# The second layer's output product by seven products instead of eight, with its weight sums made in the kernel

## The chip, the cores and the metric

The kernel runs on one core of one Trainium2 chip. The metric is the device time of one execution in microseconds; the median of three runs is given. A profile of one execution comes with it.

## The reference

The input goes through an attention step, a gated layer and a second layer. The change touches the last product of the second layer only:

```python
def _moe2_ref(x, w_in, w_out, alpha) -> np.ndarray:
    h = x @ w_in
    g = np.maximum(h, 0.0) + alpha * np.minimum(h, 0.0)
    return (g @ w_out).astype(np.float32)
```

There are 2304 tokens (18 tiles of 128), 512 model columns and 2048 hidden columns. The product `g @ w_out` is 2304 x 2048 by 2048 x 512. Weights arrive as 64-bit floating-point numbers and are turned into 32-bit ones in the kernel.

## The kernel before, in words

**Precision.** Each operand is split into a high half in TensorE's fp32r type (a ScalarE copy) and a low half, value minus high half (a subtraction on GpSimd). Each product is three matmuls: high by high, high by low, low by high (`mm3`, L487 to L490).

**Layer 2's input product** already uses seven products in place of eight (Strassen's scheme, in Winograd's form). It runs in visits: each visit takes a block of 576 tokens and a run of weight pairs `q`, and there are 32 steps of one block and one pair. A step (`step`, `close`, `prod`) has seven products of six matmuls of 288 columns. Sums of products are formed by letting ScalarE copy a finished product from one PSUM bank into another, on which the next product accumulates. After it VectorE adds and applies the activation (`close`, `prelu`, L901, L902, L909), and SyncE stores the result in the DRAM buffer `hbuf`.

**Layer 2's output product** comes after the visits. `m2_out` takes groups: for the first eight token tiles one hidden row block of 128 after the other, then the next eight tiles, then the last two tiles with four row blocks at a time, 36 groups in all. `h_load` brings 512 KB of `hbuf` (L955), `h_split` makes high halves on ScalarE (L963) and low halves on GpSimd (L964). The eight PSUM banks hold one tile each. Every token tile takes 16 x 3 matmuls of 512 columns.

**The output weights** are converted by `conv_o(q)`, one pair of row blocks each: two loads (L104), two ScalarE passes that take the bits out (`bits` L662, `top` L666), one VectorE merge of both (L670), a high half on ScalarE (L745), a low half on GpSimd (L748). In the last visit a pair is issued after each step; the last one comes after the visits.

**The order.** From the last block of layer 1 on, every engine's order is written out by the kernel. A planner holds tasks (`bg`) with an engine, an estimated cost (`COST`), dependencies and a due time. After every few matmuls `tick` moves an estimated clock and `run_bg` emits the tasks that could start about then (`LA`, `LB`, `LBD` say how far ahead). `force` emits a task that a matmul needs now. `crit` books time for work on the path that the planner does not place. `A0` is the planned time of the first step. Each engine executes what it was given in that order, so an instruction that waits holds up those behind it.

Of the kernel before, what the change touches and what calls it, by code (L numbers as in the profile page):

```python
# [8 lines left out]
F32 = mybir.dt.float32  # L9
# [14 lines left out]
def attn_moe_moe2_kernel(  # L24
# [570 lines left out]
    COST = dict(A=lambda n: 0.2 + 0.00082 * n, D=lambda n: 0.16 + 0.0011 * n, P=lambda n: 0.05 + 0.0025 * n, S=lambda n: 8.0)  # L595

    def bg(eng, n, fn, *deps, at=0.0):
        t = dict(e=eng, d=COST[eng](n) * (1.25 if eng == "D" and due[0] < A0 + 20.0 else 1.0), fn=fn, deps=deps, at=at, end=None, due=due[0])
        tasks.append(t)
        tasks.sort(key=lambda x: x["due"])  # L600
        return t

    def run_bg(flush=False):
        now = clock[0]
        busy = set()
        for t in list(tasks):
            if not flush:
                if t["e"] in busy:
                    continue
                more = 0.8 if t["due"] < now + 6.0 else 0.0  # L610
                if t["at"] > now or any(d["end"] is None or d["end"] > now + LA + more for d in t["deps"]):
                    continue
                if t["e"] != "S" and free.get(t["e"], 0.0) > now + (LBD if t["e"] == "D" and now > A0 else LB) + more:
                    busy.add(t["e"])
                    continue
            start = max([now, 0.0 if t["e"] == "S" else free.get(t["e"], 0.0)] + [d["end"] for d in t["deps"]])
            t["end"] = start + t["d"] + 0.15
            if t["e"] != "S":
                free[t["e"]] = start + t["d"]
            tasks.remove(t)  # L620
            t["fn"]()

    def force(t):
        if t["end"] is None:
            for d in t["deps"]:
                force(d)
            start = max([clock[0], free.get(t["e"], 0.0)] + [d["end"] for d in t["deps"]])
            t["end"] = start + t["d"] + 0.15
            if t["e"] != "S":
                free[t["e"]] = start + t["d"]  # L630
            tasks.remove(t)
            t["fn"]()
# [15 lines left out]
    held = dict(st0=[], st2=[], st1=[], sk=[])  # L648
# [87 lines left out]
    def conv_o(q, at):  # L736
        due[0] = A0 + 179.2 + 11.0 * q
        s = PAIR[q]
        ops = []
        for e, home in ((0, s[2]), (1, s[3])):  # L740
            z, load, bits, top, merge = unpack("o2", 2 * q + e, s[3 + e], e)

            def hi(z=z, home=home):
                z["w"] = wp.tile([128, 2, 512], F32R, tag=home, name="w2")
                nc.scalar.copy(out=z["w"][:, 0], in_=z["st"])  # L745
# [5 lines left out]
            ops.append((load, bits, top, merge, hi, lo))  # L751
        ls = [bg("S", 0, o[0], at=at) for o in ops]
        for e, (_, bits, top, merge, hi, lo) in enumerate(ops):
            st = f"st{e}"
            b_ = bg("A", 512, bits, ls[e], *held[st])
            k_ = bg("A", 512, top, b_, *held["sk"])
            m_ = bg("D", 512, merge, b_, k_)
            h_ = bg("A", 512, hi, m_)
            o_ = bg("P", 512, lo, h_)
            held[st] = [h_, o_]  # L760
            held["sk"] = [m_]
            ot[2 * q + e] = o_
# [184 lines left out]
    GROUPS = [(0, 8, [j]) for j in range(F2)] + [(8, 8, [j]) for j in range(F2)] + [(16, 2, list(range(j, j + 4))) for j in range(0, F2, 4)]  # L947
    hraw = {}
    hspl = {}
    HR, HH, HL = [[f"y{m}" for m in YO[e:e + 2]] for e in (0, 2, 4)]  # L950
# [6 lines left out]
    def h_split(u, half):  # L957
        m0, nm, js = GROUPS[u]
        if half == 0:
            hspl[u] = [p2b.tile([128, len(js), nm * 128], F32R, tag=tags[u % 2], name="hs", bufs=1) for tags in (HH, HL)]  # L960
        h, l = [t.rearrange("p j t -> p (j t)")[:, 512 * half:512 * half + 512] for t in hspl[u]]
        r = hraw[u].rearrange("p j t -> p (j t)")[:, 512 * half:512 * half + 512]
        nc.scalar.copy(out=h, in_=r)  # L963
        nc.gpsimd.tensor_sub(l, r, f32(h))  # L964

    def m2_out(u, bank):
        m0, nm, js = GROUPS[u]
        gh, gl = hspl.pop(u)
        for m in range(nm):
            if u + 1 < len(GROUPS) and m in (0, nm // 2):  # L970
                h_split(u + 1, 0 if m == 0 else 1)
            if m == nm // 2 and u + 3 < len(GROUPS):
                h_load(u + 3)
# [5 lines left out]
            if js[-1] == F2 - 1:  # L979
                os_ = (side2.tile([128, 2, HB], F32, tag="t2", name="os2", bufs=3) if m < 3 or m > 5 else  # L980
                       side2.tile([128, 2, TB], F32, tag=("sy0", "sy1", "yP5")[m - 3], name="os2", bufs=1))
                os_ = os_.rearrange("p e c -> p (e c)")[:, 0:512]
                if m % 2:
                    nc.vector.tensor_copy(os_, bank[m])  # L984
                else:
                    nc.scalar.copy(out=os_, in_=bank[m])
                r0 = (m0 + m) * 128
                nc.sync.dma_start(out=out[r0:r0 + 128, :], in_=os_)

    if True:  # L990
# [258 lines left out]
```

## Time and profile before

| | us |
|---|---|
| runs: 991.93, 992.30, 994.86; median | 992.3 |
| the profiled execution | 992.76 |
| its span, first to last instruction | 991.0 |
| TensorE busy | 951.9 |
| VectorE, GpSimd, ScalarE busy | 493.1, 457.5, 382.2 |

The span is what the trace covers; the execution's own time is 1.76 us longer. A line number in the trace is a line of the kernel. Engines are PE (TensorE), PEld (its weight loads, which overlap), DVE (VectorE), ACT (ScalarE), POOL (GpSimd) and SP (SyncE). Matmuls are pipelined: the spacing of their starts, not their duration, is what one costs.

### The profile page before, as it was taken

What the parts mean: (1) busy time and instruction counts of PE and PEld (TensorE: products, weight loads), DVE (VectorE), ACT (ScalarE), POOL (GpSimd) and SP (SyncE); (2) the same over time, 40 slices, a digit from 0 to 9 for tenths busy, and PEclk for the clock granted to TensorE, in tenths of its full rate; (3) what the DMA queues carried; (4) which work ended last, traced back from release to release, by engine and by line L of the source; (5) the groups of instructions that cost most, each with busy time, mean ns of one, the idle gap of its engine ahead of it and who ended that gap; (6) DMA issues with size and microseconds to landing.
All of it is one profiled execution on the core that took longest, in us unless ns stands there. A gap on an engine that the chain in (4) does not pass through costs nothing. (4 is left out here: it accounts for less than half of the span.)

```text
span 991.0 us, 20390 instructions
## 1 busy us (share of the span) xinstructions
PE 951.9 (96%) x8144; PEld 881.6 (89%) x8144; DVE 493.1 (50%) x990; ACT 382.2 (39%) x876; POOL 457.5 (46%) x551
## 2 busy tenths in 40 slices
PE   5689989999999999999999999999999999999998
PEld 4578889999999999999999998999999877888886
DVE  5887875455444645354541465878677730010010
ACT  4698732222222222222221556544424663232231
POOL 6488862234322243322221398854510486454543
PEclk9989899999999999999999999999999999999999
DMA  7999731132110322111101634252426763353242
GB/s 191 273 332 339 175 92 27 36 80 56 37 48 17 65 62 47 39 22 23 40 17 43 200 109 157 108 181 103 161 97 235 254 215 107 103 173 105 87 130 104
DMA packets 151702, 116.22 MB, mean 117 GB/s; under 512 B 98873, under 2 KB 130617, under 8 KB 150841
## 3 DMA queue, kind: packets, MB, share of 16 engines
q1 hardware_dynamic: 151543, 114.92, 38.6%
q8 instruction: 63, 1.03, 0.4%
q14 instruction: 32, 0.26, 0.1%
q10 hardware_dynamic: 64, 0.01, 0.0%
HBM read 86.58 MB, written 34.60 MB: 122 GB/s over the span
## 5 line engine op out<-in xcount | busy, mean ns | idle before, releaser
L964 POOL TENSOR_TENSOR hs<-hr,hs 128x512 fp32r<-128x512 f32 x72 | 93.7, 1318 | 88.5 <-ACT hs L963 86.4
L488 PE MATMUL g<-xh,w 128*128 128x288 f32 x360 | 110.1, 306 | 7.8 <-DVE u L532 3.4
L532 DVE SCALAR_TENSOR_TENSOR u<-u,g 128x288 f32<-128x288 f32 x90 | 40.7, 453 | 148.2 <-ACT u L531 148.1
L488 PE MATMUL v<-xh,w 128*128 128x288 f32 x360 | 109.7, 305 | 0.0
L489 PE MATMUL v<-xl,w 128*128 128x288 f32 x360 | 109.5, 304 | 0.0
L490 PE MATMUL g<-xh,w 128*128 128x288 f32 x360 | 107.6, 299 | 1.2 <-POOL qT L294 1.2
L490 PE MATMUL v<-xh,w 128*128 128x288 f32 x360 | 107.8, 299 | 0.9 <-POOL w L143 0.9
L489 PE MATMUL g<-xl,w 128*128 128x288 f32 x360 | 107.7, 299 | 0.0
L489 PE MATMUL y<-pl,w 128*128 128x288 f32 x336 | 99.5, 298 | 0.4 <-POOL pl L547 0.4
L490 PE MATMUL y<-ph,w 128*128 128x288 f32 x336 | 98.9, 297 | 0.0
L547 POOL TENSOR_TENSOR pl<-u,ph 128x288 fp32r<-128x288 f32 x84 | 70.4, 838 | 59.0 <-ACT ph L546 58.6
L488 PE MATMUL y<-ph,w 128*128 128x288 f32 x336 | 97.5, 302 | 0.0
L963 ACT CAST hs<-hr 128x512 fp32r<-128x512 f32 x72 | 41.7, 617 | 111.0 <-PE y L489 99.3
L531 ACT ACTIVATE u<-g 128x288 f32<-128x288 f32 x90 | 36.9, 410 | 121.0 <-PE g L490 117.5
L984 DVE COPY os<-c 128x512 f32<-128x512 f32 x5 | 3.5, 692 | 154.6 <-PE c L490 154.6
L488 PEld LDWEIGHTS g<-xh,w 128*128 128x128 f32 x360 | 68.9, 191 | 10.0 <-DVE u L532 3.8
L546 ACT CAST ph<-u 128x288 fp32r<-128x288 f32 x84 | 36.3, 432 | 90.0 <-DVE u L539 90.0
L489 PEld LDWEIGHTS v<-xl,w 128*128 128x128 f32 x360 | 69.3, 193 | 1.7
L490 PEld LDWEIGHTS v<-xh,w 128*128 128x128 f32 x360 | 69.5, 193 | 1.2 <-POOL w L143 1.2
L490 PEld LDWEIGHTS g<-xh,w 128*128 128x128 f32 x360 | 69.1, 192 | 1.4 <-POOL qT L294 1.4
L488 PEld LDWEIGHTS v<-xh,w 128*128 128x128 f32 x360 | 69.3, 193 | 0.9 <-DVE u L539 0.3
L489 PEld LDWEIGHTS g<-xl,w 128*128 128x128 f32 x360 | 69.1, 192 | 0.0
(260 smaller groups left out, 2751.7 us busy)
## 6 DMA issues: line engine op xcount, KB each, us to landing
hbuf<-t SPq DMA_DIRECT2D x64, 288.0 KB
hr<-hbuf SPq DMA_DIRECT2D x36, 512.0 KB
raw<-in_moe_w_out_dram SPq DMA_DIRECT2D x28, 512.0 KB
raw<-in_moe_w_in_dram SPq DMA_DIRECT2D x16, 512.0 KB
raw<-in_moe_w_gate_dram SPq DMA_DIRECT2D x12, 512.0 KB
raw<-in_moe_w_val_dram SPq DMA_DIRECT2D x12, 512.0 KB
vw<-vwin SPq DMA_DIRECT2D x48, 96.0 KB
sy<-y SPq DMA_DIRECT2D x8, 576.0 KB
```

What stands on the lines that cost most here:

```text
L488: nc.tensor.matmul(o, lhi, rhi, start=first, stop=False)
L489: nc.tensor.matmul(o, lhi, rlo, start=False, stop=False)
L490: nc.tensor.matmul(o, llo, rhi, start=False, stop=last)
L531: nc.scalar.activation(out=u, in_=G[:, :HB], func=AF.Tanh, scale=0.5)
L532: nc.vector.scalar_tensor_tensor(out=u, in0=u, scalar=1.0, in1=G[:, :HB], op0=ALU.add, op1=ALU.mult)
L546: nc.scalar.copy(out=ph, in_=u)
L547: nc.gpsimd.tensor_sub(pl, u, f32(ph))
L963: nc.scalar.copy(out=h, in_=r)
L964: nc.gpsimd.tensor_sub(l, r, f32(h))
L984: nc.vector.tensor_copy(os_, bank[m])
```

## The change

The 18 token tiles are divided. Four tiles (0 to 3) keep the plain product, two row blocks at a time: `prep_h` and `plain`. The other 14 form seven groups of two tiles, 256 tokens each. A group's product is a two by two block product (token tile by token tile, even row block and odd row block of a pair, left and right 256 output columns) and is computed with seven products: `prep_g`, `gprod`, `group`, `gopen`, `gclose`. Each product runs over eight row pairs with three matmuls of 256 columns. Sums of products are seeded in PSUM by ScalarE copies, as in the visits; one VectorE addition remains for each group (`row2`).

The sums of weights are made from each converted pair (`sums`, `diffs`), and their halves too (`x1`, `x2`). The sums of h are made by VectorE in place in the loaded tile (`comb`: four on each half of the contraction, 128 x 512 each). High halves stay on ScalarE. A new task kind `"V"` goes to GpSimd up to one microsecond before `B0`, about the end of the visits, and to VectorE from then on; all low halves and sums of the output product are of this kind.

Memory comes from a list of free slots (`spare`, `take`), to which the last visit's steps hand over the slots of the weights that they have used up; at most eight raw loads and five split halves of groups are held at once (`CAP`). All eight weight pairs are given to the planner at the start of the last visit. The first plain unit is put before the last step's closing products, and group 0's first product before the last plain unit. In `run_bg` the look-ahead is zero from 4 us before `A0` to 3 us after it. `m2_out`, `h_load` and `h_split` go.

```diff
--- before.py
+++ after.py
...
+    B0 = A0 + 32 * 5.6 + 1.0
+    vec = [None]
+    spare = []
...
+    def engine(t):
+        e = t["e"]
+        if e == "V":
+            e = "P" if clock[0] < B0 - 1.0 else "D"
+        vec[0] = nc.gpsimd if e == "P" else nc.vector
+        return e, COST[e](t["n"]) * (1.25 if e == "D" and t["due"] < A0 + 20.0 else 1.0)
...
+    used = dict(raw=0, ring=0)
+    CAP = dict(raw=8, ring=5)
...
+    def run_bg():
         now = clock[0]
+        la, lb = (0.0, 0.0) if A0 - 4.0 < now < A0 + 3.0 else (LA, LB)
...
+            if t["at"] > now or t["need"] > room or any(d["end"] is None or d["end"] > now + la + more for d in t["deps"]):
...
+            if e != "S" and free.get(e, 0.0) > now + (LBD if e == "D" and A0 < now < B0 else lb) + more:
+                busy.add(e)
+                continue
...
-    def conv_o(q, at):
-        due[0] = A0 + 179.2 + 11.0 * q
-        s = PAIR[q]
...
-            def lo(z=z, j=2 * q + e):
-                nc.gpsimd.tensor_sub(z["w"][:, 1], z["st"], f32(z["w"][:, 0]))
-                WO[j] = z["w"]
...
-            h_ = bg("A", 512, hi, m_)
-            o_ = bg("P", 512, lo, h_)
...
+    NM = 4
+    NG = (NT // 128 - NM) // 2
+    TG = B0 + 11.0 * NM
...
+    def conv_o(q):
+        due[0] = B0 + 11.0 * NM * q / NQ - 4.0
+        z = {}
+        tag = ("sk", "st2")[q % 2]
...
+        def hi(k):
+            def go():
+                z["s" + k] = take([128, 2, 512], F32R, "w2")[0]
+                nc.scalar.copy(out=z["s" + k][:, 0], in_=z[k])
+            return go
+
+        def lo(k):
+            def go():
+                vec[0].tensor_sub(z["s" + k][:, 1], z[k], f32(z["s" + k][:, 0]))
+                if k[0] == "w":
+                    WO[2 * q + int(k[1])] = z["s" + k]
+                if k == "w1" and q % 2:
+                    spare.append(z["back"])
+                if k == "x2":
+                    spare.append(z["xback"])
+            return go
...
+        def sums():
+            x, z["xback"] = take([128, 2, 512], F32, "st")
+            z["x1"], z["x2"] = x[:, 0], x[:, 1]
+            (a, b), (c, d), (t1, t2) = pair("w0"), pair("w1"), pair("x1")
+            vec[0].tensor_sub(t1, b, a)
+            vec[0].tensor_sub(t2, d, t1)
+
+        def diffs():
+            (a, b), (c, d), (t1, t2), (t4, t3) = pair("w0"), pair("w1"), pair("x1"), pair("x2")
+            vec[0].tensor_sub(t3, d, b)
+            vec[0].tensor_sub(t4, c, t2)
...
+        l0 = bg("S", 5.5, load(0), *ld, at=B0 - 44.0, need=1)
+        l1 = bg("S", 5.5, load(1), *ld, at=B0 - 44.0, need=1)
+        b0 = bg("A", 512, bits(0), l0, *st[0], need=more)
+        k0 = bg("A", 512, top(0), b0, *held[tag])
+        m0 = bg("D", 512, merge(0), b0, k0)
+        b1 = bg("A", 512, bits(1), l1, b0, *st[1])
+        k1 = bg("A", 512, top(1), b1, m0)
+        m1 = bg("D", 512, merge(1), b1, k1)
...
+        h0 = bg("A", 512, hi("w0"), m0, need=1)
+        h1 = bg("A", 512, hi("w1"), m1, need=1)
+        o0 = bg("V", 512, lo("w0"), h0)
+        dA = bg("V", 600, sums, m0, m1, need=1)
+        dB = bg("V", 600, diffs, dA)
+        o1 = bg("V", 512, lo("w1"), h1, o0, dB)
...
+        due[0] = TG + 1.0 * q
+        hA = bg("A", 512, hi("x1"), dB, at=B0 - 3.0, need=1)
+        oA = bg("V", 512, lo("x1"), hA)
+        due[0] = TG + 8.0 + 1.0 * q
+        hB = bg("A", 512, hi("x2"), dB, at=B0 - 3.0, need=1)
+        oB = bg("V", 512, lo("x2"), hB, oA)
+        ot[2 * q], ot[2 * q + 1] = o0, o1
+        half = lambda k, h: lambda: (z["s" + k][:, 0, 256 * h:256 * h + 256], z["s" + k][:, 1, 256 * h:256 * h + 256])
+        OX[q] = dict(P1=half("w0", 0), P2=half("w1", 0), P3=half("w1", 1), P5=half("x1", 0), P6=half("x1", 1),
+                     P4=half("x2", 0), P7=half("x2", 1))
+        ox[q] = dict(P1=o0, P2=o1, P3=o1, P5=oA, P6=oA, P4=oB, P7=oB)
...
-    GROUPS = [(0, 8, [j]) for j in range(F2)] + [(8, 8, [j]) for j in range(F2)] + [(16, 2, list(range(j, j + 4))) for j in range(0, F2, 4)]
...
-    def h_load(u):
-        m0, nm, js = GROUPS[u]
-        t = hraw[u] = p2b.tile([128, len(js), nm * 128], F32, tag=HR[u % 2], name="hr", bufs=1)
-        nc.sync.dma_start(out=t, in_=hbuf[js[0] * 128:(js[-1] + 1) * 128, m0 * 128:(m0 + nm) * 128].rearrange("(j p) t -> p j t", p=128))
...
-        nc.scalar.copy(out=h, in_=r)
-        nc.gpsimd.tensor_sub(l, r, f32(h))
...
-    def m2_out(u, bank):
-        m0, nm, js = GROUPS[u]
...
-            for e, j in enumerate(js):
+    hs = {}
+    NJ = 8 // NM
+
+    def prep_h(u):
+        due[0] = B0 + 5.5 * u - 1.7
...
+        ld = bg("S", 5.5, load, at=due[0] - 16.0, need=1)
+        h0 = bg("A", 512, hi(0), ld, at=due[0] - 8.0, need=2)
+        h1 = bg("A", 512, hi(1), h0)
+        o0 = bg("V", 512, lo(0), h0)
+        o1 = bg("V", 512, lo(1), h1, o0)
...
+    def plain(u, bank):
+        z, done = hs[u]
+        force(done)
+        gh, gl = [t[0] for t in z["s"]]
...
-                nc.sync.dma_start(out=out[r0:r0 + 128, :], in_=os_)
+            if u == F2 // NJ - 1:
+                os_ = otile()
+                nc.scalar.copy(out=os_, in_=bank[m])
+                crit("A", 512)
+                nc.sync.dma_start(out=out[m * 128:(m + 1) * 128, :], in_=os_)
...
+    GT = 20.15
+    GO = ["P1", None, None, "P6", "P2", "P7", "P5", None, "P4", "P3"]
+    GL = ["P1", None, None, "P6", "P2", "P5", "P7", "P4", "P3"]
...
+    def prep_g(g):
+        tok = (NM + 2 * g) * 128
...
+                t, R[b][f"h{r}"] = take([128, 4, 256], F32, "hr")
+                nc.sync.dma_start(out=t, in_=hbuf.rearrange("(q r p) t -> r p q t", r=2, p=128)[r][:, 4 * b:4 * b + 4, tok:tok + 256])
+                R[b][f"1{r + 1}"] = t[:, :, 0:128]
+                R[b][f"2{r + 1}"] = t[:, :, 128:256]
+            return go
...
+                zs[m, b] = t, _ = take([128, 2, 4, 128], F32R, "hs")
+                nc.scalar.copy(out=t[:, 0], in_=R[b][SRC[m]])
...
+                vec[0].tensor_sub(t[:, 1], R[b][SRC[m]], f32(t[:, 0]))
...
+        def when(m, b):
+            return TG + GT * g + (GT / 7) * ((GO if g < NG - 1 else GL).index(m) + b / 2)
...
+                h = bg("A", 512, hi(b, m), *deps, at=due[0] - 9.0, need=1, cap="ring")
+                o = bg("V", 512, lo(b, m, back), h)
...
+            due[0] = when("P1", b)
+            l0 = bg("S", 0, load(b, 0), at=due[0] - 20.0, need=1, cap="raw")
+            l1 = bg("S", 0, load(b, 1), l0, need=1, cap="raw")
+            s1 = split("P1", l0)
+            due[0] = when("P6", b) - 3.0
+            c1 = bg("V", 512, comb(b, "21", "21", "22", True), l0, l1)
+            c2 = bg("V", 512, comb(b, "11", "21", "11"), c1, *s1)
+            s6 = split("P6", c2)
+            s2 = split("P2", l1)
+            due[0] = when("P7", b) - 2.0
+            c4 = bg("V", 512, comb(b, "12", "12", "11"), c2, *s2)
+            c3 = bg("V", 512, comb(b, "11", "22", "11"), c4, *s6)
+            s7 = split("P7", c3)
+            s5 = split("P5", c1, *s7, back="h0")
+            s4 = split("P4", c3)
+            split("P3", c4, *s4, back="h1")
...
+    def gprod(o, g, m, acc):
+        zs = gs[g]
...
+                first = i + b == 0 and not acc
+                nc.tensor.matmul(o, t[:, 0, i], whi, start=first, stop=False, skip_group_check=True)
+                nc.tensor.matmul(o, t[:, 0, i], wlo, start=False, stop=False, skip_group_check=True)
+                nc.tensor.matmul(o, t[:, 1, i], whi, start=False, stop=q == NQ - 1, skip_group_check=True)
+                tick(3, 256)
+            spare.append(home)
+            used["ring"] -= 1
+
...
+    def row2(g, e):
...
+        nc.vector.tensor_add(o2, tb[:, :, :256], e.unsqueeze(1).to_broadcast([128, 2, 256]))
+        crit("D", 512)
+        nc.sync.dma_start(out=out[r0:r0 + 128, :], in_=o2)
...
+    def gclose(g):
+        tb, ac, t, b_, a, c = gset(g)
+        gprod(t, g, "P4", True)
+        row2(g, E8.pop(g))
+        gprod(c, g, "P3", True)
+        row1(g, ac[:, :, :256], 2, 0)
...
+    def gopen(g):
+        tb, ac, t, b_, a, c = gset(g)
+        gprod(t, g, "P1", False)
+        nc.scalar.copy(out=a, in_=t)
...
+    def group(g):
+        tb, ac, t, b_, a, c = gset(g)
+        if g:
+            gopen(g)
+            gclose(g - 1)
+        gprod(t, g, "P6", True)
+        nc.scalar.copy(out=b_, in_=t)
+        crit("A", 256)
+        gprod(a, g, "P2", True)
+        if g < NG - 1:
+            gprod(c, g, "P7", False)
+            e = E8[g] = side2.tile([128, HB], F32, tag="e7", name="e7", bufs=2)[:, :256]
+            nc.scalar.copy(out=e, in_=c)
+            crit("A", 256)
+            gprod(b_, g, "P5", True)
+            nc.scalar.copy(out=c, in_=b_)
+            crit("A", 256)
...
+            lastv = v == len(VISITS) - 1
+            if lastv:
+                for q in range(NQ):
+                    conv_o(q)
+                for u in range(F2 // NJ):
+                    prep_h(u)
             for q in range(q0, q1):
-                if v == len(VISITS) - 1 and q == 2:
-                    h_load(0)
-                    h_load(1)
                 step(s)
                 s += 1
-                if v == len(VISITS) - 1 and q:
-                    conv_o(q - 1, clock[0] + 0.8 + 2.4 * (q - 1))
-        h_split(0, 0)
+                if lastv:
+                    if q == 0:
+                        spare.extend((p2b, f"y{m}") for m in YO)
+                    else:
+                        spare.extend((wp, x) for x in PAIR[q - 1][2:])
+                        if q % 2 == 0:
+                            spare.append((wp, X5S[q // 2 - 1]))
+                    if q == 2:
+                        spare.extend((side2, x) for x in ("sy0", "sy1"))
+        tb, ac = SETS[0]
+        bank = [x[:, e] for y in SETS for e in range(2) for x in y]
+        plain(0, bank)
         close(len(steps) - 1)
-        h_split(0, 1)
-        h_load(2)
         prelu(len(steps) - 1, 0)
-        conv_o(NQ - 1, clock[0] + 17.6)
-        tb, ac = SETS[0]
-        bank = [tb[:, 0], ac[:, 0], Y[0][:, 0], tb[:, 1], ac[:, 1], Y[1][:, 0], Y[0][:, 1], Y[1][:, 1]]
-        for u in range(len(GROUPS)):
-            m2_out(u, bank)
...
+        for g in range(NG):
+            prep_g(g)
+        for u in range(1, F2 // NJ):
+            if u == F2 // NJ - 1:
+                gopen(0)
+            plain(u, bank)
+        for g in range(NG):
+            group(g)
...
```

## Rows read from the trace of the kernel before

**Rows 1.** The page's busy table: us, share of the span, instructions

```profile
PE 951.9 (96%) x8144; PEld 881.6 (89%) x8144; DVE 493.1 (50%) x990; ACT 382.2 (39%) x876; POOL 457.5 (46%) x551
```

**Rows 2.** Busy us (instructions) of each engine by stage, granted clock, DMA share, GB/s

```profile
640.00:738.00 98.00, 98.00 (x737) 97.84 (x736) 72.82 (x97) 40.88 (x96) 43.83 (x40) 1.00 0.38 134
738.00:785.00 47.00, 46.47 (x350) 46.24 (x349) 34.27 (x47) 23.20 (x53) 7.29 (x6) 1.00 0.65 225
785.00:840.00 55.00, 51.61 (x224) 41.04 (x224) 16.95 (x16) 29.51 (x53) 42.04 (x32) 1.00 0.55 182
840.00:980.00 140.00, 139.79 (x616) 115.12 (x615) 5.53 (x8) 33.83 (x60) 66.20 (x52) 1.00 0.39 121
```

**Rows 3.** Timeline of TensorE: start us, us, operation [idle before]

```profile
782.95 0.29 PE L886 MATMUL y<-yq,w 128*128 128x288 f32 x1
783.77 0.40 PE L884 MATMUL y<-yq,w 128*128 128x288 f32 x1 [0.53 <-ACT y L943]
...
785.48 0.40 PE L488 MATMUL c<-w,hs 128*128 128x512 f32 x1
```

**Rows 4.** Waits of TensorE from 735: us in total, times, longest

```profile
PE c L490 <- POOL hs L964: 3.0, 4, 1.1
```

**Rows 5.** Timeline of all engines at the end

```profile
986.92 0.39 PE L490 MATMUL c<-w,hs 128*128 128x512 f32 x1
987.41 0.69 DVE L984 COPY os<-c 128x512 f32<-128x512 f32 x1 [21.14 <-PE c L490]
```

**Rows 6.** Timeline of TensorE, 288-column matmuls, then 512-column ones

```profile
779.09 0.29 PE L884 MATMUL c<-yq,w 128*128 128x288 f32 x1
...
782.69 0.29 PE L884 MATMUL y<-yq,w 128*128 128x288 f32 x1
...
979.67 0.39 PE L488 MATMUL c<-w,hs 128*128 128x512 f32 x1
...
986.47 0.39 PE L488 MATMUL c<-w,hs 128*128 128x512 f32 x1
```

**Rows 7.** Instruction groups, whole span | busy us, mean ns | idle before

```profile
L901 DVE TENSOR_SCALAR t<-c,alpha 128x576 f32<-128x576 f32 x32 | 26.0, 813 | 1.3 <-PE y L886 0.7
...
L902 DVE SCALAR_TENSOR_TENSOR t<-c,t 128x576 f32<-128x576 f32 x32 | 24.2, 757 | 1.1
...
L909 DVE TENSOR_TENSOR c<-c,e 128x576 f32<-128x576 f32 x16 | 12.2, 765 | 21.0 <-PE c L886 21.0
...
L963 ACT CAST hs<-hr 128x512 fp32r<-128x512 f32 x72 | 41.7, 617 | 111.0 <-PE y L489 99.3 <-PE c L489 8.6 <-DMA hr<-hbuf 3.1
...
L666 ACT ACTIVATE sk<-raw 128x512 int32<-128x512 uint8 x32 | 21.3, 666 | 1.4 <-DVE st L670 1.4
...
L920 ACT COPY c<-c 128x288 f32<-128x288 f32 x16 | 6.2, 390 | 3.8 <-PE c L886 2.8 <-DVE t L902 1.0
...
L986 ACT COPY os<-c 128x512 f32<-128x512 f32 x5 | 2.9, 587 | 8.2 <-PE c L490 8.2
...
L748 POOL TENSOR_TENSOR w<-st,w 128x512 fp32r<-128x512 f32 x16 | 21.0, 1323 | 35.7 <-ACT w L745 35.7
...
L701 POOL TENSOR_TENSOR st<-st 128x256 f32<-128x256 f32 x3 | 2.2, 739 | 0.0
```

**Rows 8.** Single lines on VectorE: duration ns min/median/max; L670 from 640 to 700

```profile
L701 DVE TENSOR_TENSOR st<-st x5: 415/420/1398, 557.4 to 606.8; 128x256 f32<-128x256 f32 x5
...
L818 DVE TENSOR_TENSOR sy<-sy x8: 748/1054/1885, 577.7 to 683.8; 128x576 f32<-128x576 f32 x8
...
L670 DVE SCALAR_TENSOR_TENSOR st<-st,sk x3: 681/681/682, 640.1 to 651.3; 128x512 int32<-128x512 int32 x3
```

**Rows 9.** Groups of VectorE from 785 to 840

```profile
L670 DVE SCALAR_TENSOR_TENSOR st<-st,sk 128x512 int32<-128x512 int32 x11 | 13.3, 1205 | 21.9 <-ACT sk L666 21.9
```

**Rows 10.** The page's DMA issues: count, KB each

```profile
hr<-hbuf SPq DMA_DIRECT2D x36, 512.0 KB
```

**Rows 11.** Busy us of each engine at the start of the visits

```profile
598.00:610.00 12.00, 9.98 (x61) 9.07 (x59) 7.82 (x13) 7.82 (x19) 8.50 (x9) 0.86 0.66 213
```

More of the change, by code (lines that the diff above doesn't have):

```diff
@@ L601, in bg, with emit @@
         return t
-    def run_bg(flush=False):
+    def emit(t):
+        e, d = engine(t)
+        start = max([clock[0], 0.0 if e == "S" else free.get(e, 0.0)] + [x["end"] for x in t["deps"]])
+        t["end"] = start + d + 0.15
+        if e != "S":
+            free[e] = start + d
+        tasks.remove(t)
+        if t["cap"]:
+            used[t["cap"]] += 1
+        t["fn"]()
+    def run_bg():
         now = clock[0]
+        la, lb = (0.0, 0.0) if A0 - 4.0 < now < A0 + 3.0 else (LA, LB)
         busy = set()
+        kept = 0
         for t in list(tasks):
[L607 to L621, printed above, removed]
+            room = len(spare) - kept
+            if not t["cap"]:
+                kept += t["need"]
+            elif used[t["cap"]] >= CAP[t["cap"]]:
+                continue
+            e = engine(t)[0]
+            if e in busy:
+                continue
+            more = 0.8 if t["due"] < now + 6.0 else 0.0
+            if t["at"] > now or t["need"] > room or any(d["end"] is None or d["end"] > now + la + more for d in t["deps"]):
+                continue
+            if e != "S" and free.get(e, 0.0) > now + (LBD if e == "D" and A0 < now < B0 else lb) + more:
+                busy.add(e)
+                continue
+            if not t["cap"]:
+                kept -= t["need"]
+            emit(t)
     def force(t):
@@ L626, in force @@
                 force(d)
[L627 to L632, printed above, removed]
+            emit(t)
+            clock[0] = max(clock[0], t["end"])
     def crit(eng, n, ahead=0.0):
@@ L647, in attn_moe_moe2_kernel @@
     yt = {}
-    held = dict(st0=[], st2=[], st1=[], sk=[])
+    held = dict(ld=[], st0=[], st2=[], st1=[], sk=[])
     def unpack(kind, j, slot, which):
@@ L764, in attn_moe_moe2_kernel @@
+    OX, ox = {}, {}
     YO = ("P1", "P6", "P7", "P2", "P4", "P3")
@@ L957, in h_split @@
-    def h_split(u, half):
-        m0, nm, js = GROUPS[u]
[L959 to L962, printed above, removed]
-        nc.scalar.copy(out=h, in_=r)
-        nc.gpsimd.tensor_sub(l, r, f32(h))
-    def m2_out(u, bank):
[L967 to L973, printed above, removed]
-            for e, j in enumerate(js):
+    hs = {}
@@ new lines, in attn_moe_moe2_kernel, with load, flat, hi @@
+    NJ = 8 // NM
+    def prep_h(u):
+        due[0] = B0 + 5.5 * u - 1.7
+        z = {}
+        def load():
+            z["r"], z["home"] = take([128, NJ, NM * 128], F32, "hr")
+            nc.sync.dma_start(out=z["r"], in_=hbuf[u * NJ * 128:(u + 1) * NJ * 128, 0:NM * 128].rearrange("(j p) t -> p j t", p=128))
+        def flat(t, e):
+            return t.rearrange("p j t -> p (j t)")[:, 512 * e:512 * e + 512]
+        def hi(e):
+            def go():
+                if e == 0:
+                    z["s"] = [take([128, NJ, NM * 128], F32R, "hs") for k in range(2)]
+                nc.scalar.copy(out=flat(z["s"][0][0], e), in_=flat(z["r"], e))
+            return go
+        def lo(e):
+            def go():
+                vec[0].tensor_sub(flat(z["s"][1][0], e), flat(z["r"], e), f32(flat(z["s"][0][0], e)))
+                if e:
+                    spare.append(z["home"])
+            return go
+        ld = bg("S", 5.5, load, at=due[0] - 16.0, need=1)
[3 more added lines that the diff above has]
+        o1 = bg("V", 512, lo(1), h1, o0)
+        hs[u] = z, o1
@@ L975, in m2_out @@
+    def plain(u, bank):
+        z, done = hs[u]
+        force(done)
+        gh, gl = [t[0] for t in z["s"]]
+        for m in range(NM):
+            for e in range(NJ):
+                j = u * NJ + e
                 ms = slice(m * 128, (m + 1) * 128)
@@ new lines, in gprod @@
+    def gprod(o, g, m, acc):
+        zs = gs[g]
+        for b in range(2):
+            force(zs["o", m, b])
+            t, home = zs[m, b]
+            for i in range(4):
+                q = 4 * b + i
+                force(ox[q][m])
+                whi, wlo = OX[q][m]()
+                first = i + b == 0 and not acc
[5 more added lines that the diff above has]
+            used["ring"] -= 1
```

132 lines of the change are left out of this document (101 added, 31 removed).

## The prediction

> **What bounds the kernel now.** The page's busy table comes first: TensorE is busy for 96% of the span [rows 1], so the reader asks where matmul time can be taken away and where TensorE waits. The table of stages answers the second. In the 98 us of the layer-2 visits that precede the last one, TensorE never pauses, and it pauses little in the last visit; it loses 3.4 us in the 55 us after 785, where the output weights are still being converted; from 840 on it is full again [rows 2]. The stage that the change rewrites begins with the matmul at 785.48 and ends when the one at 986.92 has run, 0.23 us later: 201.7 us [rows 3, 5]. It holds 18 x 16 x 3 = 864 matmuls of 512 columns. Ten triples of them, from 979.67 to 986.47, take 6.80 us, 0.2267 us each [rows 5, 6]. 864 x 0.2267 = 195.8 us, so 5.8 us of the stage is waiting; the waits view names the GpSimd subtraction that makes the low halves of h as the longest [rows 4]. The clock is full all through these stages [rows 2]. What decides the end is therefore the number of matmuls, their pitch, and whether their operands are ready.
>
> **The matmuls.** Four tiles stay plain: 4 x 16 x 3 = 192 matmuls of 512 columns, 43.5 us. Fourteen become seven groups of two, each with 7 products x 8 row pairs x 3 = 168 matmuls of 256 columns, 1176 in all. The trace of before has no matmul of 256 columns with these operands. The nearest has 288: nine triples from 779.09 to 782.69 take 3.60 us, 0.1333 us each [rows 6]. The line through both widths is 0.0133 us plus 1/2400 us for a column, which gives 0.1200 us at 256. The bounds: 0.1333 (a narrower matmul saves nothing) and 0.1067 (the constant, which both widths show, is gone). I take 0.1200, because 256 lies only 32 columns from a measured width. Sum: 1176 x 0.1200 = 141.1 us; with the plain tiles 184.6 us, against 195.8: **-11.2 us**. A group costs 20.16 us of TensorE instead of 21.76.
>
> Each of these matmuls has its own weight load, and at 288 columns loads and matmuls run at one pace. The Trainium skill, page "TensorE: Matmul & The Clock Gate", section "LDWEIGHTS (loading the stationary operand)", prices a load at its columns over 1.2 GHz, 107 ns for 128: as long as the 256 columns themselves stream, so the narrowing uses up all the cover. By that page, section "Back-to-back issue gap", 256 columns cost 262 cycles, 109 ns, and the 1176 would cost 128.4 us, 12.7 us under my term; but it gives 518 cycles for 512 columns where the rows show 544, so the row decides.
>
> **The 5.8 us of waiting** goes with the code that waits. What comes instead is in the next two parts.
>
> **The two ends of the stage.** Before, the last step's closing product waits for ScalarE's copy: from 782.95 to 783.77, 0.82 us where a pitch is 0.13, so 0.69 us lost [rows 3]. Now the first plain unit (24 matmuls, 5.4 us) stands between the copy and that product, and covers it: **-0.7 us**. The tail: the last eviction was 512 columns on VectorE, 0.69 us [rows 5]; it becomes 256 on ScalarE, where 288 take 0.39 [rows 7]: **-0.3 us**. The last store halves too; I count nothing for it.
>
> **The start of the visits.** The new planner lets no engine queue ahead from 4 us before to 3 us after the first step. Before, 598 to 610 holds 61 matmuls where 12 us at 0.133 would hold 90, at a mean granted clock of 0.86 [rows 11]: TensorE pauses for evictions that stand behind conversion work, and after its pauses the clock is for a while at the lower of its two levels, 1.2 of 2.4 GHz. That is 29 x 0.133 = 3.9 us. Bounds: nothing gained, and all of it. The order of the work is made anew there, but the same work remains; nearer to nothing, I take **-1.0 us**.
>
> **Work for the other engines in the last visit.** A step is 42 x 0.1333 = 5.6 us. VectorE's own share of it is 2 x (0.813 + 0.757) + 0.766 = 3.91 us [rows 7]. The change opens the conversion of all eight weight pairs as soon as slots come free, which is after the first step of the last visit, and puts sums, differences and low halves on GpSimd. For a pair GpSimd has two low halves of 1.32 us [rows 7] and two pairs of 256-column sums, about 4 x 0.74 (its rows for the same sums in the earlier weights; their VectorE price is below), 5.6 us: one pair a step, and GpSimd without a pause. ScalarE has 2 x (0.67 + 0.67 + 0.62) = 3.9 us a pair beside some 1.6 us of copies: also nearly full. VectorE gets two merges. A merge took 0.68 us with GpSimd idle and 1.21 us in the stretch where GpSimd was busy for 42 of 55 us [rows 2, 8, 9]. So a step asks 3.91 + 2 x 0.68 = 5.3 us of VectorE at best and 3.91 + 2 x 1.21 = 6.3 at worst, against 5.6. Behind a late merge stand the sums and the activation of the previous step, and TensorE waits for these before it starts a product in the same banks; five products lie between, so the first 1.6 us are free. Some six steps are loaded so: 0 to 6 x 0.7 = 4.3 us. I take **+2.5 us**, nearer to the contended row. The output pairs done by the end of the visit: about 33 us / 5.6, minus the first h unit, five of eight.
>
> The same lock in the notes: the Trainium skill, page "SBUF — State Buffer", section "Who interferes with whom", says that a VectorE instruction with two SBUF inputs and a GpSimd instruction that reads SBUF exclude each other for the whole instruction. The trace agrees [rows 8, 9].
>
> **The plain tiles and the groups.** From the planner's time B0 on, all this work goes to VectorE and GpSimd gets none, so uncontended rows apply: 0.42 us for 256 columns, 0.75 for 576 [rows 8], on that line about 0.68 for 512. Three pairs are left, each 2 merges, 2 low halves and 4 sums, 2 x 0.68 + 2 x 0.68 + 4 x 0.42 = 4.4 us: 13 us. Fourteen halves of h: 9.5. Sixteen low halves of sums: 10.9. That is 34 us of 43.5, and the pairs are some five units ahead. A group then has 14 low halves, 8 sums and one eviction: 22 x 0.68 + 0.77 = 15.7 us of VectorE in 20.16. ScalarE has 14 x 0.62 + 4 x 0.39 + 0.59 = 10.8 us. Neither binds, so these are priced at nothing while TensorE covers them. Loads are 28 of 512 KB in 141 us, and before there were 36 of that size in the stage [rows 10]: about 104 GB/s, below the 121 that the stage moved from 840 to 980 [rows 2]. SyncE's queue holds them in one order with the output stores; a store waits for its eviction, and a load behind it is asked for some 20 us early. What remains is the start of the groups, where each half is asked for only some 3.6 us ahead and needs about 1.5 us on two engines. Bounds: none (as in the visits) to 3.4 us per 55 us as in the conversion stretch, 11 us over the whole stage; I take **+2.0 us**, since only the first third resembles that stretch.
>
> **The sum.** 991.0 - 11.2 - 5.8 - 0.7 - 0.3 - 1.0 + 2.5 + 2.0 = 976.5 us of span. The profiled execution's own time was 992.76, 1.76 us over its span and 0.46 above the median of the runs; so 978.3 for that execution and **978 us** for the median.
>
> **The rivals.**
> *Weights late.* The last visit is overloaded on three engines at once, and pairs are not ready when the plain units ask. For it: the 1.21 us merges and the old stretch's waits on GpSimd. Against: the pairs are due one every 5.4 us only from the end of the visit on, and about five are done then. Price: 4.3 us instead of 2.5, and two pairs a whole chain late, 0.67 + 0.67 + 1.21 + 0.62 + 1.32 = 4.5 us each: about 11 us more, 989; a mild case gives 984.
>
> *The narrow matmul saves nothing.* If loads or issue set the pitch and 256 columns still take 0.1333 us, the 1176 cost 156.8 us, 15.7 more: 994, on the border to no change. It decides from 0.132 us on. Against it: 288 and 512 columns lie on one line with the full clock's slope.
>
> *VectorE sets the groups (the other side).* If its 512-column operations cost there what a contended merge cost, 1.21 us, a group asks 22 x 1.21 + 0.77 = 27.4 us of VectorE, 7.2 more than TensorE, seven times: about 1028, slower. It binds from 0.88 us and cancels the gain from 0.97. Against it: no GpSimd work is left in the groups, and the clean rows stand at 0.68.
>
> *The constant goes.* If the 0.0133 us that both widths carry were no part of a 256-column matmul, the 1176 would cost 125.4 us, 15.7 less: 962. Against it: it is the same at 288 and 512 columns. The 109 ns of the Trainium skill's section on the issue gap, named above, lies near this case, and the rows so far do not bear it out.
>
> **How the numbers follow.** The forecast holds with 0.64 (972 to 983); weights late 0.15 (984 to 990); no gain from narrowness 0.07; VectorE as the bound 0.07; the constant gone 0.03; the rest, 0.04, is divided. The range 971 to 990 leaves out the slow matmul, the VectorE bound, the lost constant and the tails. Differences under 0.3%, 3 us, can't be told from none. Faster: 0.64 + 0.14 + 0.03 and a little of the rest, 0.82; within 0.3%: 0.06, from the pitch rival and late weights at their worst; slower: 0.12, from VectorE, half of the pitch rival and the rest.
>
> **What the profile would show.** Right: 256-column matmuls 0.120 us apart; groups of about 20.2 us with no wait on VectorE; GpSimd idle after about 785; a stage of 185 to 190 us; merges above 1 us in the last visit and waits of 2 to 3 us there. Wrong: a pitch of 0.13; TensorE waiting once or more per group for a low half; the first plain units stopping for weights; or a last visit longer than before by over 5 us.

## The result

The changed kernel takes 980.57 us (median of 4 runs, 979.40 to 982.01) against 992.12 (4 runs, 990.57 to 994.86): ratio 0.9881, 95% interval 0.9856 to 0.9907 (ratios here are always to the kernel before). 978 was forecast, with a range of 971 to 990. The profiled execution took 980.62 us; its span is 978.8, 12.2 less than before.

The stages of the changed kernel, in the columns of [rows 2] (PE, PEld, DVE, ACT, POOL, granted clock, DMA share, GB/s):

```profile
600.00:640.00 40.00, 35.49 (x261) 34.56 (x261) 31.71 (x39) 24.60 (x56) 31.70 (x28) 1.00 0.35 121
640.00:738.00 98.00, 98.00 (x738) 97.98 (x737) 72.33 (x95) 42.97 (x100) 44.16 (x42) 1.00 0.39 137
738.00:785.00 47.00, 45.69 (x344) 45.44 (x342) 37.70 (x49) 27.31 (x60) 23.11 (x22) 1.00 0.66 224
785.00:830.00 45.00, 44.49 (x218) 37.61 (x217) 38.76 (x70) 31.06 (x57) 3.38 (x3) 1.00 0.65 226
830.00:972.00 142.00, 140.86 (x1150) 139.24 (x1148) 104.95 (x166) 69.55 (x137) 0.00 (x0) 1.00 0.39 120
```

TensorE's timeline at the start of the plain tiles, two matmuls of a group's product, and the last one:

```profile
786.73 0.40 PE L488 MATMUL c<-w,hs 128*128 128x512 f32 x1
...
973.08 0.28 PE L1189 MATMUL y<-w,hs 128*128 128x256 f32 x1
...
974.52 0.28 PE L1189 MATMUL y<-w,hs 128*128 128x256 f32 x1
...
975.47 0.28 PE L1191 MATMUL y<-w,hs 128*128 128x256 f32 x1
```

From 973.08 to 974.52 lie twelve starts: 0.1200 us each, the forecast pitch to the last digit. The stage, with the last step's closing products in it, took 204.1 us before (from 783.08, when the last step's own products end, to 987.15; [rows 3, 5]) and takes 188.9 now (786.73 to 975.59): 15.2 us less, where 15.7 were forecast (11.2 + 5.8 + 0.7 - 2.0). GpSimd is idle from 788.4 on, inside the first plain unit. The tail from the last matmul to the end falls from 3.85 to 3.2 us.

The rest of the span goes the other way. The first step starts 1.1 us later; nothing before it was rewritten, and the kernels below start it anywhere from 600.6 to 602.9. From there to the end of the last step's own products it takes 184.6 us instead of 182.0. TensorE's waits from 590 on, in the form of [rows 4]:

```profile
PE c L994 <- DVE t L1012: 2.5, 1, 2.5
PE c L994 <- ACT c L1053: 1.7, 2, 1.3
PE y L1191 <- DVE hs L1142: 1.6, 4, 0.7
PE c L994 <- DVE u L539: 1.4, 1, 1.4
```

L994 is a matmul of the visits, L1012 VectorE's activation, L1053 a ScalarE copy between PSUM banks, L1191 a matmul of the groups and L1142 a low half for it. Only the third line belongs to the stage that was rewritten. The fourth stood in the kernel before too (1.4 us). The first two lie in the visits and are new or longer.

The groups of VectorE and ScalarE from 830 to 972:

```profile
L1142 DVE TENSOR_TENSOR hs<-hr,hs 128x512 fp32r<-128x512 f32 x96 | 63.9, 688 | 30.7 <-ACT hs L1136 29.6
L1149 DVE TENSOR_TENSOR hr<-hr 128x512 f32<-128x512 f32 x55 | 37.1, 687 | 0.6
...
L1136 ACT CAST hs<-hr 128x512 fp32r<-128x512 f32 x96 | 55.4, 622 | 11.8 <-DVE hr L1149 6.6 <-PE c L1191 1.5 <-DVE hs L1142 1.5
```

The stage from 860 to 960, in the columns of the stages above:

```profile
860.00:960.00 100.00, 100.00 (x837) 100.00 (x836) 73.54 (x116) 48.40 (x95) 0.00 (x0) 1.00 0.39 120
```

VectorE's 512-column operations cost 0.69 us, against 0.68 by the line through the rows of [rows 8]. It is busy for 73.5 of 100 us; TensorE never pauses.

### The profile page after: what moved, and what is told of

The parts are those of the page before. It is cut to its first block, busy times and chain, and to the rows that moved or that the text cites. A ratio compares the mean times of both kernels' runs of the same rounds, so it can differ in the third digit from the quotient of the medians.

```text
span 978.8 us, 21665 instructions
## 1 busy us (share of the span) xinstructions
PE 938.3 (96%) x8648; PEld 895.0 (91%) x8648; DVE 617.0 (63%) x1199; ACT 421.7 (43%) x965; POOL 365.7 (37%) x486
## 4 chain that ended last, share of the span: by engine, by line
PE 76%; DMA 6%; DVE 5%; POOL 4%; ACT 3%; issue 3%; SPq 2%; DVEq 0%; POOLq 0%; ACTq 0%
PE y L488 4%; PE g L488 4%; PE v L489 4%; PE v L488 4%; PE y L490 4%; PE y L489 4%; PE v L490 4%; PE g L489 4%; PE g L490 4%; PE y L995 3%; PE y L994 3%; PE c L994 3%; PE y L996 3%; PE c L995 3%; PE c L996 3%
## 5 line engine op out<-in xcount | busy, mean ns | idle before, releaser
L1142 DVE TENSOR_TENSOR hs<-hr,hs 128x512 fp32r<-128x512 f32 x98 | 65.3, 688 | 31.2 <-ACT hs L1136 30.1
L488 PEld LDWEIGHTS v<-xh,w 128*128 128x128 f32 x360 | 68.3, 190 | 1.2 <-DVE u L539 0.5
L490 PEld LDWEIGHTS v<-xh,w 128*128 128x128 f32 x360 | 68.4, 190 | 0.0
L488 PEld LDWEIGHTS y<-ph,w 128*128 128x128 f32 x336 | 62.2, 189 | 4.7 <-issue 4.4
L539 DVE SCALAR_TENSOR_TENSOR u<-u,v 128x288 f32<-128x288 f32 x90 | 40.6, 451 | 39.0 <-PE v L490 38.1
```

The costliest lines, as they stand in the source:

```text
L488: nc.tensor.matmul(o, lhi, rhi, start=first, stop=False)
L490: nc.tensor.matmul(o, llo, rhi, start=False, stop=last)
L539: nc.vector.scalar_tensor_tensor(out=u, in0=u, scalar=0.5, in1=G[:, :HB], op0=ALU.mult, op1=ALU.mult)
L1142: vec[0].tensor_sub(t[:, 1], R[b][SRC[m]], f32(t[:, 0]))
```

## The experiments

All are timed against the kernel before on the same chip, where its median was 992.06 to 992.60 us; two runs that are compared with each other were not always on one chip. They go from the visits to the stage itself, and end with two that put gains together.

**The start of the visits.** Two kernels, the changed one without the zero window and the one before with it:

```diff
-        la, lb = (0.0, 0.0) if A0 - 4.0 < now < A0 + 3.0 else (LA, LB)
+        la, lb = LA, LB
```

> The changed kernel with the look-ahead left as it was around the first step (the zero window taken out, nothing else). My theory: in the zero window the 256-column sums on VectorE fall beside GpSimd subtractions, and each waits for a whole one (1.39 to 1.66 us instead of 0.42); VectorE is late and TensorE waits 2.5 us. Without the window those sums take about 0.42 again, the 2.5 us wait goes, the clock dip of the kernel before may come back: about 979.5 us (978.5 to 980). Rival, as predicted: the window gains 1 us, so 981.5 without it. Second rival: no difference, 980.6.

> The kernel before with only the zero look-ahead window added. My theory: the same late VectorE sums appear at the start of the visits, TensorE waits 2 to 3 us there, and the time is about 1 us longer, 993.1. Rival, as predicted: 1 us shorter, 991.1.

Measured: 978.68 us (4 runs, ratio 0.9863, interval 0.9850 to 0.9877) without the window, and 994.37 against 992.2 (ratio 1.0022, 1.0010 to 1.0033) with it in the kernel before. So the window costs 2.2 us in the kernel before; in the changed kernel the medians say 1.9, but the two intervals overlap. The last pair of experiments has the same line changed with the pause of the next paragraph gone: 980.13 us with the window and 977.07 without, in ranges that do not meet (976.70 to 977.50 and 978.97 to 980.83). The forecast had the window gain 1.

What was forecast does happen. In the run without the window ScalarE's copy (L1030) stands behind the conversion's passes and is made at 605.96, and TensorE waits for it:

```profile
606.40 0.40 PE L994 MATMUL c<-yq,w 128*128 128x288 f32 x1 [1.22 <-ACT c L1030]
```

With the window the copy is made at 604.30, this wait is gone, and the first 42 matmuls of the visits (as many as one step has) take 8.4 us instead of 10.2. But the next 42 take 8.4 instead of 5.6. VectorE's timeline in the changed kernel shows why; L730 to L737 are 256-column sums of the input weights:

```profile
608.78 1.39 DVE L730 TENSOR_TENSOR st<-st 128x256 f32<-128x256 f32 x1
610.20 1.54 DVE L731 TENSOR_TENSOR st<-st 128x256 f32<-128x256 f32 x1
611.66 1.66 DVE L736 TENSOR_TENSOR st<-st 128x256 f32<-128x256 f32 x1
613.36 1.54 DVE L737 TENSOR_TENSOR st<-st 128x256 f32<-128x256 f32 x1
```

GpSimd's timeline in the same stretch:

```profile
608.54 1.35 POOL L726 TENSOR_TENSOR w<-st,w 128x512 fp32r<-128x512 f32 x1 [1.87 <-PE c L996]
609.85 3.19 POOL L921 TENSOR_TENSOR yq<-sy,yq 128x576 fp32r<-128x576 f32 x2
613.00 3.17 POOL L928 TENSOR_TENSOR sy<-sy 128x576 f32<-128x576 f32 x2
```

And VectorE's in the run with the look-ahead kept:

```profile
607.77 1.39 DVE L730 TENSOR_TENSOR st<-st 128x256 f32<-128x256 f32 x1
609.20 0.43 DVE L731 TENSOR_TENSOR st<-st 128x256 f32<-128x256 f32 x1
609.54 0.42 DVE L736 TENSOR_TENSOR st<-st 128x256 f32<-128x256 f32 x1
609.99 0.43 DVE L737 TENSOR_TENSOR st<-st 128x256 f32<-128x256 f32 x1
```

In the window the four sums fall beside GpSimd instructions that follow each other without a gap, and each sum waits for the end of a whole one: 6.1 us together. With the look-ahead kept, GpSimd pauses after the first (until 610.14, when three of the four are done), and they take 2.7. VectorE's addition and activation for the previous step stand behind them, and TensorE waits 2.5 us for these. In the kernel before with the window the same four sums take 1.40, 1.54, 1.65 and 1.53 us, and the same wait appears:

```profile
616.87 0.40 PE L885 MATMUL c<-yq,w 128*128 128x288 f32 x1 [2.33 <-DVE t L903]
```

The price differs from execution to execution, and the granted clock goes with it. The first 1176 of the 1344 matmuls of the visits take 161.3 us in all five traces without the window. With it they take 162.2 in three traces of the changed kernel and its variants, where the clock is 1.00 from 600 to 640, and 163.5 to 163.7 in four others, where TensorE runs for some us at the lower of its two levels after the long wait. The stretch in one of these, the run of the next paragraph:

```profile
600.00:640.00 40.00, 35.62 (x250) 34.95 (x251) 30.37 (x38) 23.97 (x55) 30.21 (x26) 0.96 0.31 108
```

Two more with the window, where the lower level comes before the long wait, take 162.8 and 163.0. So by the traces the window costs 0.9 to 2.4 us, the more where TensorE is at the lower level after the wait.

**The pause in the last visit.** One number:

```diff
-        l0 = bg("S", 5.5, load(0), *ld, at=B0 - 44.0, need=1)
+        l0 = bg("S", 8.0, load(0), *ld, at=B0 - 44.0, need=1)
```

(and `l1` alike).

> The changed kernel, with the planner's estimate of a weight load in the last visit raised from 5.5 to 8 us. My theory: the 1.3 us pause of TensorE near 770 comes from ScalarE, which stands 1.4 us behind a weight load that landed later than planned and then makes its PSUM copy late; with a later start of the conversion that wait goes: about 979.4 us, no pause near 770. Rival: the contended merges are the cause and the pause stays, 980.6. Second rival: the pairs come so much later that the plain tiles wait instead: 982 or more.

ScalarE's timeline in the changed kernel, where the pause stands:

```profile
766.74 0.62 ACT L810 CAST w<-st 128x512 fp32r<-128x512 f32 x1 [0.19 <-DVE st L803]
768.77 0.68 ACT L790 ACTIVATE st<-raw 128x512 f32<-128x512 f32 x1 [1.41 <-DMA raw<-in_moe_w_out_dram]
769.35 0.38 ACT L1049 COPY e<-c 128x288 f32<-128x288 f32 x1
769.63 0.66 ACT L796 ACTIVATE sk<-raw 128x512 int32<-128x512 uint8 x1
770.19 0.40 ACT L1053 COPY c<-c 128x288 f32<-128x288 f32 x1
```

The load was asked for at 763.84 (SyncE's queue had held it behind an `hbuf` store that waits for VectorE) and is used at 768.77. ScalarE stands 1.4 us for it, the copies behind it are late, and TensorE has no matmul start between 769.04 and 770.64. With 8 us booked, TensorE is full in that visit:

```profile
738.00:785.00 47.00, 47.00 (x355) 47.00 (x354) 36.52 (x50) 26.91 (x59) 20.84 (x21) 1.00 0.66 226
```

980.13 us (ratio 0.9876, 0.9861 to 0.9891): the pause is gone, but alone the time can't be told from 980.57. In this trace the lower clock at the start of the visits takes back what the pause gave. The merges are less contended as well (0.73 us on the mean against 1.01), so it is the chain in the changed kernel's trace, and not this run, that tells the load from the rival.

**What the engine did alone.** The kernel before with the low halves on VectorE:

```diff
-        nc.gpsimd.tensor_sub(l, r, f32(h))
+        nc.vector.tensor_sub(l, r, f32(h))
...
-            o_ = bg("P", 512, lo, h_)
+            o_ = bg("D", 512, lo, h_)
```

(and the subtraction in `conv_o` alike).

> The kernel before with the low halves of h and of the output weights on VectorE instead of GpSimd; the products stay. My theory: the 5.8 us of waiting in the old stage come from GpSimd's 1.3 us subtractions and the merges that stand behind them, so most of it goes without any change to the products: about 987.5 us (986.5 to 989). Then some 5 of the measured 11.5 us are the engine's and the rest the seven products'. Rival: the waiting comes from late loads and the chain of a conversion, and stays: 992.

989.63 us (11 runs, ratio 0.9974, 0.9965 to 0.9983): 2.6 us, half of what was expected. The stage falls from 201.7 to 199.2 us, and no TensorE wait on a low half is left in it. What stays of the 5.8 us is spread over the stage's start, two evictions and a few matmuls between 804 and 825, none over 0.6 us. So 2.6 of the 11.5 us, less than a quarter, are had without any change to the products.

**Doubling VectorE's work in the groups.**

```diff
                 vec[0].tensor_sub(t[:, 1], R[b][SRC[m]], f32(t[:, 0]))
+                vec[0].tensor_sub(t[:, 1], R[b][SRC[m]], f32(t[:, 0]))
```

(in the other run only where `b` is 1).

> The changed kernel with each low half of a group subtracted twice over (the same values written again), so 36 VectorE operations of 512 columns for a group instead of 22. My theory: VectorE is hidden under TensorE as long as a group asks it for less than 20.16 us. Now it asks 36 x 0.64 to 0.69 + 0.69 = 23.7 to 25.5 us, so it sets the pace, seven times 3.6 to 5.4 us: 1006 to 1018 us, with TensorE waiting for low halves all through the groups. Rival: the look-ahead of five halves hides it, under 985.

> The changed kernel with the low halves of the second half of the contraction subtracted twice: 29 VectorE operations for a group, 19.3 to 20.7 us against TensorE's 20.16. My theory: this lies at the break point, so nothing or little: 980.6 to 985. Rival: VectorE is already the hidden bound in the groups, and each added operation shows: 7 x 7 x 0.65 = 32 us more, 1012.

1016.99 us (2 runs) and 983.27 (0.9909, 0.9894 to 0.9923). The stage from 860 to 960 with all low halves doubled:

```profile
860.00:960.00 100.00, 87.64 (x679) 82.42 (x678) 96.20 (x151) 39.02 (x77) 0.00 (x0) 1.00 0.33 101
```

TensorE's waits in it:

```profile
PE c L1192 <- DVE hs L1143: 7.4, 12, 1.5
PE y L1192 <- DVE hs L1143: 4.4, 7, 1.5
```

The same stage with half of them doubled:

```profile
860.00:960.00 100.00, 99.97 (x835) 99.76 (x834) 95.45 (x150) 48.10 (x94) 0.00 (x0) 1.00 0.39 119
```

With 29 operations for a group VectorE is busy for 95 us of 100 and TensorE still does not wait; with 36 VectorE is full and TensorE waits 19 times, 11.8 us. The break point lies between, as the sum had it. The 2.7 us more of the run with 29 are lost in group 0 and in the last group, by its trace: its stage is 191.7 us against 188.9.

**The whole of it on one engine.** First GpSimd, then VectorE:

```diff
-            e = "P" if clock[0] < B0 - 1.0 else "D"
+            e = "P"
```

(in the second run `e = "D"`).

> The changed kernel with the whole new kind of task on GpSimd, also after the visits: what VectorE does in the plain tiles and groups goes to GpSimd. My theory: 22 operations of 1.3 us are 28.6 us for a group against 20.16 of TensorE, seven times 8.4 us, and the plain tiles lose some 13 more: about 1050 us, slower than before the change. Rival: VectorE's share wasn't needed, GpSimd keeps up: under 985.

> The changed kernel with the whole new kind of task on VectorE from the start, also in the last visit. No merge then meets a GpSimd instruction there. My theory: the lock cost little in the last visit, and VectorE has only 1.7 us a step to spare there, so the pairs come later and the plain tiles wait some: 981 to 986. Rival: the lock is what the last visit pays for, and without it the time falls to 979 or less.

On GpSimd: 1082.65 us (one run). The stage from 860 to 960:

```profile
860.00:960.00 100.00, 78.65 (x522) 73.66 (x521) 2.07 (x3) 33.15 (x62) 92.19 (x75) 0.84 0.33 101
```

GpSimd's subtraction in its groups:

```profile
L1142 POOL TENSOR_TENSOR hs<-hr,hs 128x512 fp32r<-128x512 f32 x64 | 81.1, 1281 | 16.5 <-ACT hs L1136 16.3
```

22 operations of 1.28 us are the forecast 28 us for a group; the last six groups take 31.3 us each, and GpSimd stands some 3.4 us in each for high halves from ScalarE. TensorE, which waits all through, is granted 0.84 of full speed on the mean, between its two levels. How much of the loss beyond the forecast (1082.65 against 1050) is the clock's is not shown. On VectorE: 982.59 (0.9901, 0.9884 to 0.9917), not to be told from 980.57. The last visit is better there (TensorE busy for 46.68 us of 47), the first group worse (a wait of 2 us for ScalarE): what GpSimd takes off VectorE and what the lock costs may cancel, but the times don't show it.

**Fewer plain tiles.**

```diff
-    NM = 4
+    NM = 2
```

> The changed kernel with two plain tiles and eight groups instead of four and seven. TensorE's work falls by another 1.6 us. The plain tiles then last 21.8 us instead of 43.5. My theory: these 43.5 us are what VectorE needs for the weight sums; some 34 us of it are left at the end of the visits (4.7 pairs of 4.4, low halves of h, 10.9 for the halves of sums), and group 0 asks for 15.7 more, about 50 us against 42 until the end of group 0: some 8 us of waiting, about 987 us. Rival: the cover is ample and the fewer matmuls show: 979.

990.16 us (10 runs, 0.9977, 0.9965 to 0.9989). TensorE from 785 to 830:

```profile
785.00:830.00 45.00, 38.17 (x195) 31.28 (x194) 42.12 (x74) 30.61 (x58) 3.74 (x3) 0.96 0.57 197
```

It loses 6.8 us of 45, waiting for `w` and `hs` (4.0 us on VectorE, 2.9 on ScalarE's high halves), while VectorE is busy for 42. The 1.6 us that the count of matmuls saves are lost several times over, and three more than the forecast 987: the plain tiles are the time in which the weight sums are made. A plain unit also takes four row blocks in this run instead of two (`NJ`); what that does is not told apart.

**The order at the joint.**

```diff
-        plain(0, bank)
         close(len(steps) - 1)
+        plain(0, bank)
```

> The changed kernel with the last step's closing products ahead of the first plain unit again, as before the change. My theory: the closing product waits 0.5 us and TensorE loses 0.7 us, as in the kernel before: about 981.3 us, and the wait shows near 786. Rival: nothing is lost, or the later plain unit gains the preparation as much: 980.6.

979.81 us (979.60 to 982.80; 0.9886, 0.9869 to 0.9904): no difference that these runs can show. The wait is there,

```profile
789.97 0.40 PE L994 MATMUL y<-yq,w 128*128 128x288 f32 x1 [0.53 <-ACT y L1053]
```

but the groups then wait less (0.7 us in all against 1.6), and the stage takes 188.5 us against 188.9. By the traces the covered pause had been given back a few units later.

**Put together.** The first run has the window's line and the two loads changed as above; the second has besides:

```diff
-        due[0] = TG + 1.0 * q
+        due[0] = TG - 12.0 + 1.0 * q
...
-        due[0] = TG + 8.0 + 1.0 * q
+        due[0] = TG - 4.0 + 1.0 * q
```

> The changed kernel with the look-ahead kept around the first step and the weight load booked at 8 us. My theory: the two gains add, 1.9 us and about 0.5 to 1.3 us: 977.5 to 978.5 us, with neither the 2.5 us wait near 617 nor the pause near 770. Rival: the second gain is given back in the groups, 978.7 as with the first alone.

> The same as the run with both, and the halves of the weight sums due 12 us earlier, so that VectorE makes them inside the plain tiles and not between the first halves of group 0. My theory: the four to five short waits of TensorE for low halves between 828 and 845, some 2 us, go: 976 to 977 us. Rival: VectorE has no room in the plain tiles, and a plain unit or group 0 waits as long: 978.

Both corrections: 977.07 us (4 runs, 976.70 to 977.50; 0.9852, 0.9838 to 0.9865), below both kernels. TensorE has one kind of wait left from 735 on:

```profile
PE y L1191 <- DVE hs L1142: 1.5, 3, 0.7
```

With the halves of the weight sums due earlier as well: 980.83 (0.9882, 0.9865 to 0.9899). Group 0 waits longer, now on ScalarE (2.5 us) as well as on VectorE (1.4): it seems that the work brought forward pushed the group's own first halves back; which instruction did so was not followed up.

## Why the prediction was right, and where it was not

By the traces the stage gave 15.2 us (15.7 forecast), the tail 0.6 (0.3), the last visit cost 1.7 (2.5), the start of the visits 0.9 where a gain of 1.0 was forecast, and the first step started 1.1 us later, which varies from execution to execution and had no term. The span was 2.3 us above the forecast 976.5.

**The matmuls, -11.2.** Right as a term: the pitch at 256 columns is 0.1200 us. Neither of the two pitch rivals holds. The 262 cycles, 109 ns, that the Trainium skill gives for 256 columns in "TensorE: Matmul & The Clock Gate", section "Back-to-back issue gap" (there the gap of an isolated matmul) are not what this kernel's 256-column matmuls show; the constant of 0.0133 us stays at the narrowest width too.

**The 5.8 us of waiting, and +2.0 in its place.** Right in sum: the stage is 188.9 us where the matmuls alone, with the closing products, need 186.2, so 2.7 us wait or run late, most of it in group 0 as forecast. The run with the engine alone puts 2.6 of the old 5.8 us on GpSimd; the rest went with the old code.

**The two ends, -0.7 and -0.3.** The pause is covered, as forecast, but with it back the stage is no longer, so the 0.7 is no gain. The tail gave 0.6, twice the term: the last store, counted as nothing, is smaller too.

**The start of the visits, -1.0.** This step failed, in its sign. Its mechanism is there: the copy no longer stands behind conversion work, and the first 42 matmuls gain 1.7 us. What it did not count is VectorE: short sums that wait for whole GpSimd instructions, 2.8 us lost in the next 42. [rows 8] had the sign of it: the slowest of five 256-column sums took 1.40 us there, where the median took 0.42. It also took the low clock of [rows 11] for a part of the loss. The kernel before and its variant with the low halves on VectorE need 10.2 us each for those 42, the one granted 0.86 from 598 to 610, the other 1.00: the slower TensorE waits less for the copy, 0.43 us against 1.20.

**The last visit, +2.5.** Near in size, 1.7 by the traces, by luck: the cause was another. GpSimd was to work without a pause, a pair a step, with five pairs done; it is busy for 23 of 47 us, makes the sums of three pairs, and its first low half comes at 759.7, because the weights come later than counted: the visit's first loads are asked for at 746.6 and used from 753.6 on. The merges are contended (eight of them, 1.01 us on the mean), but TensorE's one pause there, 1.3 us where 2 to 3 were expected, follows ScalarE's wait for the late load. The 0.68 us of [rows 8] was read as a merge beside an idle GpSimd; two of those three start together with a GpSimd subtraction, which then takes 1.85 us where 1.3 is usual, so the row shows merges that came first. Weights late, the first rival, did not occur with four plain tiles and did with two.

**VectorE in the groups.** 22 operations of 0.69 us, as costed, hidden under 20.16 us of TensorE. The rival's break point of 0.88 us an operation is the same as 29 operations at 0.69; there TensorE does not yet wait in the middle of the stage.

What is still open: what makes the clock fall after the window's wait in some executions and not in others, and how the lock and the late load share the 1.7 us of the last visit.

## What to carry to other kernels

When seven products replace eight, count what the narrower matmul costs by a line through measured widths, and then count the sums on the engine that makes them: the exchange holds only while a group's sums cost less than its matmuls, and plain work must stand where the first sums are made. A change of a planner's look-ahead is a change of its own and wants its own measurement: the wait that it removes in one step can come back, longer, in the next. A covered pause is a gain only if the wait behind it does not grow.

## What the runs showed of the hardware that was not expected

A short VectorE addition beside an unbroken row of GpSimd subtractions costs as much as a long one: 1.39 to 1.66 us for 256 columns that take 0.42 alone. So in such a row the price of the lock goes by the number of VectorE instructions, not by their size. The Trainium skill's rule on this, in "SBUF — State Buffer", section "Who interferes with whom", fits: the loser waits for the whole instruction.

The lower clock is not always a loss: ahead of a copy that TensorE waits for anyway, it cost nothing in the kernel before (10.2 us for the first 42 matmuls of the visits with it and without); after the wait that the window brings, it went with some 1.4 us more (163.5 to 163.7 against 162.2). With everything on GpSimd, TensorE was granted 0.84 over 100 us and was busy for 78.65 us with 522 matmuls, which need 62.6 us at a pitch of 0.1200. Whether that cost time is not shown, since GpSimd was busy for 92 of these 100 us.
